# Loading q and k of two blocks in fp32, scores in 64x64 tiles, and a fixed table of orders, in a windowed-attention and SwiGLU kernel

## The chip, the cores and the metric

The kernel runs on one core of one Trainium2 chip. The metric is the device time of one execution in microseconds. It is given as the median of runs, and a profiled execution gives the time and order of every instruction.

## What is computed

```python
# q, k, v: (4, 8, 768, 64) fp32; window = 128, n_sink = 4
scores = (q @ k.T) / sqrt(64)
keep = (key < 4) | ((0 <= query - key) & (query - key < 128))
a = softmax(where(keep, scores, -1e9))
x = (a @ v), heads laid side by side          # 3072 tokens x 512
xn = x / sqrt(mean(x * x) + 1e-6) * rms_g
out = (silu(xn @ w_gate) * (xn @ w_val)) @ w_out   # 512 -> 1536 -> 512
```

## The kernel before

The 768 positions of each of the four batches are cut into six blocks of 128, so that there are 24 blocks g, with t = g % 6 the place in the batch. For a block of 128 keys, the scores are made transposed, keys on the partitions, against the 256 queries of the block itself and the next one: `scores(g)` (line 457) issues eight matmuls of 256 columns, one for each head, two heads at a time on the upper and lower 64 rows of the array. The last block of a batch (`scores_last`, line 475) has 128 columns only. ScalarE takes the exponent out of PSUM (`exps`, line 510), VectorE multiplies by a 0/1 mask (`mask_dve`, line 522, two instructions per block of 128x1024 elements) or, from block 16, GpSimd selects (`mask_pool`, line 535). Blocks 0 and 1 get their mask as a matmul into PSUM beforehand (`mask_bias`, line 447). The sinks are scored for several blocks at once in four column tiles of 32 (`sink_s`, line 668). `av` (line 548) multiplies by v, with a column of ones that gives the sums; `normal`, `square` and `rms` (lines 575 to 616) normalise. x is transposed by TensorE for the first eight blocks and by DMA after.

The FFN takes groups G of four blocks (512 tokens). Group 0 is cut in four chunks of 128 tokens, groups 1 and 2 in two of 256, the others are whole. `ffn` (line 938) issues the gate and value matmuls of one chunk and one set of feature tiles, 16 or 8 or 4 matmuls each, about 0.87 us; ScalarE and VectorE make the hidden tile; `project` (line 892) multiplies by w_out.

q and k of block 0 come in fp32 by SyncE and are cast on the chip. All other q, k, v and all weights are cast by DMAs that GpSimd issues, in the order of `LOADS` (line 186): q and k of block 1, v of block 0, two weight loads, and so on.

What runs when on each engine is set at build time. Every step is registered by `op` with its engine, cost, needs and PSUM banks, and `Plan.run` (line 70) simulates the engines with these costs and always takes the step that can start first. On the chip the five engines then run their lists in order and wait for one another by semaphores. 30 matmuls on zeros (`warm`) are fillers that the planner puts where TensorE has nothing else.

Of the kernel before, what the change touches and what calls it, by code (L numbers as in the profile page):

```python
# [25 lines left out]

class Plan:
# [6 lines left out]
    RESERVE = 8  # L34
# [15 lines left out]
    def land(self, ring, first, work):  # L50


        r = self.rings
        if ring == "POOL":
            begin = max(first, r["POOL"], r["HW"])
            r["POOL"] = begin + (1.4 * work if begin < 8500 else work)
            self.loads -= 1
            return r["POOL"] + 520
        if ring == "HW":
            begin = max(first, r["HW"])  # L60
            r["HW"] = begin + (1.25 * work if begin > 2500 else work)
            return r["HW"] + 900
        begin = max(first, r["TR"], r["POOL"])
        if self.loads:
            r["POOL"] = max(r["POOL"], first) + work
            work *= 2
        r["TR"] = begin + work
        return r["TR"] + (350 if ring == "TR" else 650)

    def run(self):  # L70
        free, users = dict(self.START), {}
        self.loads = sum(o["ring"] == "POOL" for o in self.ops)
        wait = {o["at"]: set(o["needs"]) for o in self.ops}
        cand = {e: [] for e in free}
        left = len(self.ops)
        for o in self.ops:
            for t in o["needs"]:
                users.setdefault(t, []).append(o)
            if not o["needs"]:
                for e in o["ways"]:  # L80
                    cand[e].append(o)
        busy, warm, mode, order = [], False, 0, []
        while left:
            first = None

            many = min(
                (o for o in cand["PE"] if len(o["takes"]) > self.RESERVE), default=None,
                key=lambda o: o["prio"],
            )
            for e, found in cand.items():  # L90
                for o in found:
                    k = len(o["takes"])
                    if k > len(self.banks):
                        continue
                    ready = o["ready"] + self.HOP[e] if o["ready"] else 0
                    if k:
                        ready = max(ready, sorted(self.banks.values())[k - 1] + 40)
                    start = max(free[e], ready)
                    if (k and many and o["prio"] > many["prio"] and start > many["ready"]
                            and len(self.banks) - k < len(many["takes"])):  # L100
                        continue
                    key = (start, o["prio"], ready, o["at"])
                    if first is None or key < first[0]:
                        first = key, e, o
            if first is None:
                raise RuntimeError("stuck: %s" % [
                    (o["gives"], list(wait[o["at"]])) for o in self.ops if o["at"] in wait
                ][:20])
            (start, *_), e, o = first
            for x in o["ways"]:  # L110
                cand[x].remove(o)
            wait.pop(o["at"])
            left -= 1
            ns, lat, fn = o["ways"][e]
            if e == "PE":
                busy = [(a, d) for a, d in busy if a > start - 3413]
                warm = start - free[e] < 4000 and (warm or sum(d for a, d in busy) > 3000)
                ns = ns if warm else 2 * ns
                if o["mode"] != mode:
                    ns, mode = ns + 110, o["mode"]  # L120
                busy.append((start, ns if mode != 2 else 0))
                lat = ns + 180
# [6 lines left out]
            if o["ring"] is not None:  # L129
                end = self.land(o["ring"], end, o["work"]) + self.LATE  # L130
            for s in o["drops"]:
                self.banks[self.held[s]] = end + 12
            for t in o["gives"]:
                for x in users.pop(t, ()):
                    x["ready"] = max(x["ready"], end + 12)
                    w = wait[x["at"]]
                    w.discard(t)
                    if not w:
                        for way in x["ways"]:
                            cand[way].append(x)  # L140
            order.append((start, end, e, fn, o))
        return order


@with_exitstack
def kernel(
# [30 lines left out]
    HW = 4 * VW  # L177
    SW = P // HP
    inv_sqrt_d = 1.0 / math.sqrt(D)
    F32_LOADS = ("ks0","qs0")  # L180
# [4 lines left out]
    DEPTH = 8  # L185
    LOADS = "q-1 k-1 v-0 w-0-2 v-1 qkv-2 qkv-3 w-2-4 w-4-6 w-6-8 w-8-9 w-9-10 w-10-12 qkv-4 wo-0-6 qkv-5 wo-6-12 qkv-6 qkv-8 qkv-7"
    LOADS += "".join(f" qkv-{g}" for g in range(9, NB))
    PE_MASKS = 2
    POOL_MASK_FROM = 16
# [73 lines left out]
    dve(130, lambda: nc.vector.memset(bias.bitcast(I32), 0), gives=["bias0"], prio=-98)  # L263
    for b in range(B):
        dve(60, lambda b=b: nc.vector.memset(V16[b][:, :, :, D:VW], 1.0),
# [49 lines left out]
    dve(220, cut_ident, ["ident"], ["idnos"], -59)  # L315
    dve(700, make_masks, [("bias", 0), ("bias", 1)], ["masks"], MASKS_PRIO)
    dve(300, make_sel, ["ident"], ["sel", "headm"], MASKS_PRIO + 1)
# [27 lines left out]
    for i, name in enumerate(F32_LOADS):  # L345
# [3 lines left out]
           (), [(n + "st", g)], -90 + i, ring="HW", work=970)  # L349
# [10 lines left out]
    def sw_load(fn, gives, work, ns=870, needs=()):  # L360
        n = len(issue)
        more = [("sw", n - DEPTH)] if n >= DEPTH else []
        op({"POOL": (ns, 1900, fn)}, list(needs) + more, list(gives) + [("sw", n)], -89 + n,
# [3 lines left out]
    def sw_block(g, what="qkv"):  # L367
        for n in what:
            needs = [("s", g - LOAD_LEAD)] if g >= LEAD_FROM else []
            if n == "v":  # L370
                sw_load(lambda g=g: load_v(g), [("v", g)], 910, needs=needs)
# [29 lines left out]
    def warm(i):  # L401
        ps = bank(("warm",)) if i == 0 else BANK[("warm",)]
        nc.tensor.matmul(out=ps[:, 0:P], lhsT=zeros, rhs=zeros, start=True, stop=True)

    for i in range(WARM):
        pe(55, lambda i=i: warm(i), ["zeros"] + ([("warm", i - 1)] if i else []),
           [("warm", i)], 1e9, takes=[("warm",)] if i == 0 else (),
           drops=[("warm",)] if i == WARM - 1 else ())
# [7 lines left out]
    pe(1000, unit_gb, ["ones", "grow"], ["gbm"], GB_PRIO, takes=[("gb",)], mode=2)  # L416
# [71 lines left out]

    def exps_last(g, hi):
        if ("el", g) not in T:  # L490
            T["el", g] = epool.tile([P, H, P], BF16, name="e0", bufs=3)
        nc.scalar.activation(
            out=T["el", g][:, hi * HP:(hi + 1) * HP, :].rearrange("p x c -> p (x c)"),
            in_=BANK.pop(("s", g, hi)), func=ACT.Exp, scale=inv_sqrt_d,
        )

    def mask_dve_last(g, hi):
        ev = T["el", g][:, hi * HP:(hi + 1) * HP, :]
# [4 lines left out]
    def mask_pool_last(g, hi):  # L503
        ev = T["el", g][:, hi * HP:(hi + 1) * HP, :]
# [5 lines left out]
    def exps(g, u, hi, n0, n1, last):  # L510
        if ("e", g, u) not in T:
            T["e", g, u] = epool.tile([P, 4, 2, P], BF16, name=f"e{u}", bufs=3)
        ps = BANK[("s", g, u, hi)]
        if last:
            BANK.pop(("s", g, u, hi))
        nc.scalar.activation(  # L516
            out=T["e", g, u][:, 2 * hi:2 * hi + 2, n0:n1, :].rearrange("p x n c -> p x (n c)"),
# [4 lines left out]
    def mask_dve(g, u):  # L522
        t = g % NT
        nq = 2 if t + 1 < NT else 1
        et = T["e", g, u]
        m = masks[:, 0 if t == 0 else 1, 0:nq, :]
        if nq == 2:
            ev = et.rearrange("p x n c -> p x (n c)")
            mv = m.rearrange("p n c -> p (n c)").unsqueeze(1).to_broadcast((P, 4, nq * P))
        else:  # L530
            ev = et[:, :, 0, :]
            mv = m.to_broadcast((P, 4, P))
        nc.vector.tensor_tensor(out=ev, in0=ev, in1=mv, op=ALU.mult)  # L533

    def mask_pool(g, u, n):
        et = T["e", g, u][:, :, n, :]
        if n == 0:
            nc.gpsimd.affine_select(  # L538
                out=et, in_=et, compare_op=ALU.is_ge,
                fill=0.0, base=0, pattern=[[0, 4], [1, P]], channel_multiplier=-1,  # L540
            )
        else:
            nc.gpsimd.affine_select(
                out=et, in_=et, compare_op=ALU.is_ge,
                fill=0.0, base=-1, pattern=[[0, 4], [-1, P]], channel_multiplier=1,
            )

    def av(g, u):
# [7 lines left out]
        for j in range(2):  # L556
            for hi in range(2):
                h = 4 * u + 2 * j + hi
                x = 2 * hi + j
                dest = pv[:, (h - 4 * u) * VW:(h - 4 * u + 1) * VW]  # L560
                if t >= 1:
                    nc.tensor.matmul(  # L562
                        out=dest, lhsT=T["e", g - 1, u][:, x, 1, :],
# [3 lines left out]
                own = (T["e", g, u][:, x, 0, :] if t + 1 < NT  # L567
                       else T["el", g][:, hi * HP + 2 * u + j, :])
                nc.tensor.matmul(  # L569
                    out=dest, lhsT=own, rhs=V16[b][:, t, h, :],  # L570
                    start=(t == 0), stop=True, skip_group_check=True,
                )
        T.pop(("e", g - 1, u), None)

    def normal(g, u):
        if u == 0:
# [127 lines left out]
    def block_scores(g):  # L704
# [10 lines left out]
        for n0, n1 in parts:  # L715
            needs = [("kT", g)] + [("qT", g + i) for i in range(n0, n1)] + gate_of(g)
            needs += [("mb", g)] if g < PE_MASKS else []
# [20 lines left out]
            for u in range(2):  # L738
                for hi in range(2):
                    act(215 * (n1 - n0) + 55,  # L740
                        lambda g=g, u=u, hi=hi, n=(n0, n1), last=last: exps(g, u, hi, *n, last),
                        [("s", g, n0), "table"] + ([("av", g - 2, u)] if g >= 2 else [])
                        + ([("x", g, u, 0, n0)] if hi else []),
                        [("x", g, u, hi, n) for n in range(n0, n1)], early,
                        drops=[("s", g, u, hi)] if last else ())
        for u in range(2):
# [3 lines left out]
            elif g < POOL_MASK_FROM or t == 0:  # L750
                dve(600 if nq == 2 else 335, lambda g=g, u=u: mask_dve(g, u),
                    sum(xs, []) + ["masks"], [("e", g, u)], early)
                es = [[("e", g, u)]] * nq
            else:
                es = []
                for n in range(nq):
# [268 lines left out]
```

## Time and profile before

| | us |
|---|---|
| Runs (3) | 245.65, 244.9, 246.14; median 245.65 |
| Span of the profiled execution, first to last instruction (the only time that its page gives) | 243.9 |
| TensorE busy | 235.3 |
| VectorE busy | 181.1 |
| ScalarE busy | 131.2 |
| GpSimd busy | 89.5 |
| DMA, share of 16 engines' span: GpSimd's queue, SyncE's queue | 80.6%, 28.6% |

The granted TensorE clock is 1.000 over the span. A span of an engine's instruction includes its pipeline: matmuls overlap, so that their busy time is a union and not a sum of column times. PE is TensorE, PEld its weight loads, DVE VectorE, ACT ScalarE, POOL GpSimd, SP SyncE.

### The profile page before, as it was taken

To read this page: it belongs to the slowest core of one execution; us is meant where nothing else is said; L and a number is where in the kernel's file an instruction comes from. 1 tells how busy PE (TensorE), PEld (TensorE's weight loads), DVE (VectorE), ACT (ScalarE), POOL (GpSimd) and SP (SyncE) were. 2 spreads that over 40 slices of the span, in tenths; PEclk is the share of its full clock that TensorE was granted. 3 is DMA by queue.
4 is the path that set the end of the run, shared out by engine and by line. 5 is a ranking of instruction groups with operands and counts; after the bars stand their busy time and mean duration, and the time that the engine had idled before them with its cause. 6 is when DMAs were issued, how large, how long until landed. Compare 5 with 4: busy or idle time off the path is not lost.

```text
span 243.9 us, 5513 instructions
## 1 busy us (share of the span) xinstructions
PE 235.3 (96%) x2116; PEld 148.4 (61%) x2116; DVE 181.1 (74%) x481; ACT 131.2 (54%) x268; POOL 89.5 (37%) x116
## 2 busy tenths in 40 slices
PE   4988999999999999999999999999999999999994
PEld 2558987884788875587786544544554444444443
DVE  4279979896999999999899789896379760377700
ACT  4686565769684827584844574572553311333111
POOL 8976785596435546344520130321320000000000
PEclk9999999999999999999999999999999999999999
DMA  9999999999999999999999461110231002200022
GB/s 127 151 167 196 186 187 187 159 133 163 141 194 162 155 154 156 162 225 137 128 131 143 110 171 25 22 22 21 91 108 24 1 0 86 86 3 0 0 86 86
DMA packets 113579, 27.35 MB, mean 112 GB/s; under 512 B 103697, under 2 KB 110609, under 8 KB 113554
## 3 DMA queue, kind: packets, MB, share of 16 engines
q0 software_dynamic: 81760, 13.90, 80.6%
q1 hardware_dynamic: 31650, 12.99, 28.6%
q8 instruction: 16, 0.26, 0.4%
q10 hardware_dynamic: 144, 0.13, 0.2%
q14 instruction: 9, 0.07, 0.1%
HBM read 28.31 MB, written 6.29 MB: 142 GB/s over the span
## 4 chain that ended last, share of the span: by engine, by line
PE 76%; DMA 15%; DVE 4%; POOL 2%; issue 1%; POOLq 0%
PE v L863 23%; PE g L863 22%; PE o L896 20%; DMA wv<-in_moe_w_val_dram 7%; DMA q<-in_q_dram 5%; PE s L468 3%; DMA v<-in_v_dram 3%; PE av L569 2%; PE av L562 1%; PE av L552 1%; PE o_last L914 1%; DVE e L533 1%; DVE x L581 1%; POOL wg L381 1%; POOL wv L381 1%
## 5 line engine op out<-in xcount | busy, mean ns | idle before, releaser
L863 PE MATMUL v<-xnt,wv 128*128 128x128 bf16 (+2 forms) x528 | 71.1, 282 | 0.0
L863 PE MATMUL g<-xnt,wg 128*128 128x128 bf16 (+2 forms) x528 | 69.8, 282 | 0.3 <-DMA wg<-in_moe_w_gate_dram 0.2
L870 ACT ACTIVATE th<-g 128x512 bf16<-128x512 f32 x72 | 43.2, 600 | 50.0 <-PE g L863 47.4
L896 PE MATMUL o<-wo,hT 128*128 128x512 bf16 x276 | 65.4, 379 | 0.0
L876 DVE SCALAR_TENSOR_TENSOR p<-th,g 128x512 bf16<-128x512 bf16 x72 | 47.9, 682 | 21.6 <-ACT th L870 21.4
L863 PEld LDWEIGHTS <-wg 128*128 128x128 bf16 x528 | 43.1, 98 | 19.7 <-DMA wg<-in_moe_w_gate_dram 0.6
L863 PEld LDWEIGHTS <-wv 128*128 128x128 bf16 x528 | 43.1, 98 | 19.2 <-issue 0.5
L886 DVE TENSOR_TENSOR hT<-p,v 128x512 bf16<-128x512 bf16 x72 | 47.1, 680 | 1.5 <-PE v L863 0.7
L516 ACT ACTIVATE e<-s 128x512 bf16<-128x512 f32 (+1 forms) x88 | 43.8, 569 | 7.2 <-PE s L468 5.8
L896 PEld LDWEIGHTS <-hT 128*128 128x128 bf16 x276 | 25.3, 98 | 26.5 <-issue 1.5
L904 ACT ACTIVATE osb<-o 128x512 f32<-128x512 f32 x23 | 13.8, 601 | 23.4 <-PE o L896 23.4
L335 POOL DMA_DIRECT2D k<-in_k_dram x23 | 20.4, 886 | 16.3 <-DMA v<-in_v_dram 11.3
L339 POOL DMA_DIRECT2D v<-in_v_dram x24 | 21.3, 886 | 11.6 <-DMA q<-in_q_dram 10.5
L335 POOL DMA_DIRECT2D q<-in_q_dram x23 | 20.5, 891 | 11.7 <-DMA k<-in_k_dram 4.0
L581 DVE TENSOR_TENSOR x<-av,rden 128x256 bf16<-128x256 f32 x48 | 20.4, 424 | 1.7
L589 ACT ACTIVATE sq<-x 128x512 bf16<-128x512 bf16 x24 | 15.1, 630 | 11.4 <-DVE x L581 11.3
L613 DVE SCALAR_TENSOR_TENSOR xr<-x,r,gb 128x512 bf16<-128x512 bf16 x24 | 18.0, 751 | 0.9
L533 DVE TENSOR_TENSOR e<-e,masks 128x1024 bf16<-128x1024 bf16 x26 | 17.0, 684 | 1.4 <-ACT e L516 1.4
L538 POOL TENSOR_SCALAR_AFFINE_SELECT e<-e 128x512 bf16<-128x512 bf16 x10 | 6.4, 637 | 31.6 <-ACT e L516 16.1
L569 PE MATMUL av<-v,e 128*128 128x65 bf16 x192 | 17.1, 193 | 0.4 <-ACT e L516 0.3
L562 PE MATMUL av<-v,e 128*128 128x65 bf16 x160 | 15.1, 193 | 0.0
L569 PEld LDWEIGHTS <-e 128*128 128x128 bf16 x192 | 13.0, 97 | 3.3 <-ACT e L516 0.7
(75 smaller groups left out, 181.1 us busy)
## 6 DMA issues: line engine op xcount, KB each, us to landing
out_dram<-osb SPq DMA_DIRECT2D x23, 256.0 KB, 2.3
v<-in_v_dram POOLq DMA_DIRECT2D x24, 128.0 KB, 11.7
q<-in_q_dram POOLq DMA_DIRECT2D x23, 128.0 KB, 12.5
k<-in_k_dram POOLq DMA_DIRECT2D x23, 128.0 KB, 11.8
wo<-in_moe_w_out_dram POOLq DMA_DIRECT2D x2, 768.0 KB, 11.1
wg<-in_moe_w_gate_dram POOLq DMA_DIRECT2D x5, 256.0 KB, 7.7
wv<-in_moe_w_val_dram POOLq DMA_DIRECT2D x5, 256.0 KB, 8.1
stage<-in_k_dram SPq DMA_DIRECT2D x1, 256.0 KB, 3.3
```

The costliest lines, as they stand in the source:

```text
L335: nc.gpsimd.dma_start(out=T[name, g], in_=block_of(src, g))
L339: nc.gpsimd.dma_start(out=V16[b][:, t, :, 0:D], in_=block_of(v, g))
L516: nc.scalar.activation(out=T["e", g, u][:, 2 * hi:2 * hi + 2, n0:n1, :].rearrange("p x n c -> p x (n c)"), in_=ps.rearrange("p (j c) -> p ...
L533: nc.vector.tensor_tensor(out=ev, in0=ev, in1=mv, op=ALU.mult)
L569: nc.tensor.matmul(out=dest, lhsT=own, rhs=V16[b][:, t, h, :], start=(t == 0), stop=True, skip_group_check=True,)
L581: nc.vector.tensor_tensor(out=T["x16", g][:, 4 * u:4 * u + 4, :], in0=pvv[:, :, 0:D], in1=rden.unsqueeze(2).to_broadcast((P, 4, D)), op=AL ...
L613: nc.vector.scalar_tensor_tensor(out=T["xr", g], in0=T.pop(("x16", g)).rearrange("p h d -> p (h d)"), scalar=r[:, 3:4], in1=gb, op0=ALU.mu ...
L863: nc.tensor.matmul(out=ps[:, i * n:(i + 1) * n], lhsT=w_sb[:, kt, ft * P:(ft + 1) * P], rhs=T["xnt", G][:, kt, cols], start=(kt == 0), sto ...
L870: nc.scalar.activation(out=T["th", key], in_=BANK[("g", key)], func=ACT.Tanh, scale=0.5,)
L876: nc.vector.scalar_tensor_tensor(out=T["p1", key], in0=T.pop(("th", key)), scalar=1.0, in1=BANK.pop(("g", key)), op0=ALU.add, op1=ALU.mult,)
L886: nc.vector.tensor_tensor(out=T[hk][:, i:i + n, cols], in0=T.pop(("p1", key)).rearrange("p (n c) -> p n c", n=n), in1=BANK.pop(("v", key)) ...
L896: nc.tensor.matmul(out=BANK[("o", G, tb)], lhsT=T["h", G, ft // 4][:, ft % 4, tb * P:(tb + 1) * P], rhs=wo[:, ft, :], start=(ft == 0), sto ...
```

## The change

Five things change.

1. q and k of blocks 0 and 1 are loaded in fp32, k by SyncE's queue and q by ScalarE's, and cast on the chip. GpSimd no longer loads q and k of block 1.
2. For blocks g >= 4 that are neither first nor last of their batch (13 of them: 4, 7 to 10, 13 to 16, 19 to 22), the scores are made in 64x64 tiles. Keys 0 to 63 of the block need queries 0 to 191, keys 64 to 127 need queries 64 to 255; the last 64 queries of these are put where the first 64 of the others would be. So a head takes three matmuls, of 192, 64 and 128 columns, and ScalarE reads 384 columns per bank instead of 512. The masks put the moved part in its place: two VectorE instructions per block (128x512 and 128x1536), or four GpSimd selects.
3. One tile `e` holds the exponents of all eight heads of a block, where there were two, and a third kind for the last blocks.
4. The order of each engine's steps is read from a table, `ORDER`, in place of the planner's choice. The planner still hands out PSUM banks, with other costs.
5. Each of the 30 fillers takes a bank of its own for itself.

```diff
-    F32_LOADS = ("ks0","qs0")
+    F32_LOADS = ("ks0", "qa0", "ks1", "qa1")
...
-    LOADS = "q-1 k-1 v-0 w-0-2 v-1 qkv-2 qkv-3 w-2-4 w-4-6 ..."
+    LOADS = "v-0 w-0-2 v-1 qkv-2 qkv-3 w-2-4 w-4-6 ..."
+    TRI_FROM = 4
...
+    def tri_scores(g):
+        b, t = divmod(g, NT)
+        qkT = T["qkT", b]
+        for hp in range(HP):
+            u, j = divmod(hp, 2)
+            for kh, c0, q0, n in ((0, 0, 0, TW), (1, 0, TW, DH), (1, DH, DH, P)):
+                for hi in range(2):
+                    pr = slice(hi * D, (hi + 1) * D)
+                    slot = ("s", g, u, hi)
+                    if slot not in BANK:
+                        bank(slot)
+                    k0, q1, o = t * P + kh * DH, t * P + q0, j * TW + c0
+                    nc.tensor.matmul(
+                        out=BANK[slot][kh * DH:(kh + 1) * DH, o:o + n],
+                        lhsT=qkT[pr, 1, hp, k0:k0 + DH], rhs=qkT[pr, 0, hp, q1:q1 + n],
+                        start=True, stop=True, tile_position=(hi * D, kh * DH),
+                        skip_group_check=True,
+                    )
+
+    def tri_exps(g, u, hi):
+        x = HP * hi + 2 * u
+        nc.scalar.activation(
+            out=e_tile(g)[:, x:x + 2, 0:TW],
+            in_=BANK.pop(("s", g, u, hi))[:, 0:2 * TW].rearrange("p (j c) -> p j c", c=TW),
+            func=ACT.Exp, scale=inv_sqrt_d,
+        )
+
+    def tri_mask(g):
+        et = e_tile(g)
+        m = masks[:, 1].rearrange("p n c -> p (n c)")
+        for out, in0, in1 in (
+            (slice(TW, 2 * P), slice(0, DH), slice(TW, 2 * P)), (slice(0, TW),) * 3,
+        ):
+            nc.vector.tensor_tensor(
+                out=et[:, :, out], in0=et[:, :, in0],
+                in1=m[:, in1].unsqueeze(1).to_broadcast((P, H, in1.stop - in1.start)),
+                op=ALU.mult,
+            )
...
+        elif t and g >= TRI_FROM:
+            tri_block(g)
         else:
             block_scores(g)
...
-    order = plan.run()
+    order = plan.run(ORDER)
```

(DH is 64 and TW is 192.) The table counts the steps in the order of their registration. Read back into names, it begins so, with mb for the mask bias, T for a transpose, S for scores (S0.0 and S0.1 against the block itself and the next), VS for a sink product, AV for the two halves of the value product, X for the transpose of x:

```
PE:   7 fillers, mb0, gain broadcast, Tq0, Tk0, filler, Tq1, filler, S0.0, S0.1, filler, Tk1,
      2 fillers, Tq2, filler, AV0.1, VS0.0, filler, AV0.0, mb1, Tq3, filler, S1.0, S1.1, 2 fillers,
      VS0.1, filler, Tk2, 3 fillers, AV1.1, X0, AV1.0, filler, S2, gate 0-3 of chunk 0, sink scores,
      3 fillers, value 0-3 of chunk 0, X1, Tk3, ...
ACT:  load q0, load q1, activation table, cast q0, gain, copy Tq0, copy Tq1, exps of block 0, ...
DVE:  constants, masks, cast k0, cast q1, copy Tk0, cast k1, copy Tk1, copy Tq2, ...
POOL: identity, bias, k2, q2, v0, q3, v1, gate 2-3, value 0-1, gate 0-1, value 2-3, k3, v2,
      gate 6-7, gate 4-5, value 6-7, value 4-5, the other weights up to value 8, q4, q5, k4, v3, ...
SP:   gain row, load k0, load k1, ...
```

## The prediction

> **What bounds the kernel now.** First the page's busy times, then the same by stage, then the timeline of the first 34 us, then the chain of waits.
>
> ```profile
> PE 235.3 (96%) x2116; PEld 148.4 (61%) x2116; DVE 181.1 (74%) x481; ACT 131.2 (54%) x268; POOL 89.5 (37%) x116
> ```
>
> TensorE is busy for 96% of the span, but starts are overlapped and ends modelled, so I ask where its work is thin:
>
> ```profile
> 0.00:6.00 6.00, 2.87 (x14) 1.59 (x15) 2.73 (x16) 2.46 (x3) 4.79 (x11) 1.00 1.02 127
> 6.00:12.00 6.00, 6.00 (x42) 3.64 (x40) 1.52 (x4) 3.73 (x12) 5.98 (x8) 1.00 1.69 151
> 12.00:18.00 6.00, 4.95 (x78) 3.50 (x77) 4.21 (x18) 4.88 (x16) 4.57 (x7) 1.00 2.18 165
> 18.00:24.00 6.00, 5.32 (x95) 4.59 (x94) 5.46 (x16) 4.14 (x11) 3.97 (x6) 1.00 1.45 197
> 24.00:36.00 12.00, 11.74 (x203) 10.98 (x200) 9.74 (x22) 6.59 (x13) 9.57 (x12) 1.00 1.70 187
> ...
> 60.00:80.00 20.00, 20.00 (x212) 15.80 (x210) 19.18 (x52) 14.04 (x31) 9.01 (x11) 1.00 1.87 171
> 80.00:100.00 20.00, 20.00 (x196) 13.60 (x194) 18.86 (x55) 12.09 (x26) 11.37 (x13) 1.00 1.87 157
> ```
>
> Columns: stretch, length, busy time and instructions of PE, PEld, DVE, ACT, POOL, then clock, DMA share, GB/s. PE is full from about 24 us; VectorE is at 94 to 96% between 60 and 100. The thin part is the start: 14 matmuls in 6 us, then 42 and 78. Listing the distances between matmul starts after 46 us, I find none that exceeds the streaming of its columns by more than 0.17 us; nearly all of the excess is 0.09 to 0.11 us on each side of a change of the array's shape. So two things can move the end: when the start fills PE, and how much PE work there is.
>
> ```profile
> 7.24 2.07 PE L411 MATMUL gb<-grow,ones 1*128 1x512 f32 x2
> ...
> 9.24 1.04 PE L468 MATMUL s<-qkT 64*128 64x128 bf16 x16
> ...
> 11.37 1.39 PE L450 MATMUL s<-bias,ident 128*128 128x512 bf16 x4
> ...
> 12.59 0.42 PE L569 MATMUL av<-v,e 128*128 128x65 bf16 x8
> ...
> 17.06 0.40 PE L628 MATMUL x<-ident,xr 128*128 128x128 bf16 x4 [0.61 <-DVE xr L613]
> ```
>
> Columns: start, length in us, engine, line, operation, count. Block 0's scores wait behind the gain broadcast at 7.24, its value product (12.59) behind block 1's mask bias (11.37), and the transpose of x for block 0 comes at 17.06. The first FFN group starts at 19.69.
>
> ```profile
> 15.69 8.13 DMA wv<-in_moe_w_val_dram
> ...
> 24.11 8.46 DMA wv<-in_moe_w_val_dram
> ...
> 65.48 0.22 PE ss L671 x4
> ...
> 80.84 0.33 PE s L484 x8
> ...
> 91.05 0.54 PE s L468 x8
> ```
>
> The chain says the same: until 32.57 (24.11 + 8.46, the last gate and value weights land) it runs through DMAs, then through PE to 240.57. The last 3.3 us (output half, VectorE copy, store) the change leaves alone.
>
> **The change, part by part.** *Start, block 0.* The new PE table puts the gain broadcast and mask bias before the transposes of q and k of block 0, and block 0's value product before block 1's bias. It can: POOL makes the identity and the bias before any load (here one load issue of 1.01 us comes first, and the identity only at 2.42), so that block 0's mask bias, here at 4.16, can start near 2.5. That takes 2.07 us (7.24 to 9.24) out from between the transposes and the scores, and 1.2 us (11.37 to 12.59) out from before the value product. Against it: the gain row goes first on SP and holds k0's issue for 0.47 us; DVE casts q1 before it copies k0's transpose, so block 0's scores wait behind q1's landing, with four fp32 loads in flight. In this trace the first four loads (k0, q0 by SP, q1, k1 by POOL) land at 4.15, 5.42, 6.30 and 7.08, about 1.0 us each; I take the fourth near 7.5 and the first scores near 8.8, 0.4 us earlier instead of 2. The value product then follows the scores by some 2 us (one half's exps, 4 x 0.4 us on ACT) instead of 3.35, near 10.9, 1.7 us earlier; x of block 0 shifts from 17.06 to about 15.4 and the FFN's input to about 16.8.
>
> *Start, weights.* The four weight loads of columns 0 to 4 land, by the trace, at 11.20, 12.53, 19.80 and 21.23, behind ten q, k, v loads on POOL and two on SP. The new table has five on POOL and four on the hardware queues ahead, three blocks fewer. The six blocks between 13.65 and 18.84 took 0.87 us each, so the fourth lands near 18.6 and the third near 17.3. The first FFN group starts at about 17.4, 2.3 us earlier. But all weights land behind eleven blocks instead of twelve: 32.57 becomes about 31.7, 0.9 us earlier, and the new order can run 12 FFN groups before it needs that one, as many as ran by 32.62 here. So the lead carried past the weights is between 0.9 and 2.3 us; I take 1.4, nearer the lower end, since the weights bind last. Below nothing: if four fp32 loads at once push q1 and k1 back by 2 us, the lead is lost, 0. The casts add two VectorE copies of about 0.6 us (the ACT cast is 0.618); they lie in the stretch where VectorE is busy 1.52 of 6 us. ACT's two DMA issues (0.45 to 0.56 each on SP) come before its 1.28 us table load and end near 3.1, before any data lands at 4.15: nothing. What is late next if the cover fails is the copy of k0's transpose.
>
> The Trainium skill, page "DMA: Bandwidth & Descriptors" (section "Issuing engines are not separate DMA queues"), says that issuing on two queues saves issue time alone, because all share the same 16 engines. By it the two-queue part would be worth nothing in transfer time. No run here has two hardware queues loading at once, and the sum above takes nothing from the second queue.
>
> *Scores in 64x64 tiles.* Thirteen blocks (4, 7 to 10, 13 to 16, 19 to 22) go from 8 matmuls of 256 columns to 24 of 192, 64 and 128. The chain prices the old form: 0.54 us with its change of shape, and 0.33 for 8 matmuls of 128 columns. So 128 columns in each of four pairs cost 0.21 us and the fixed part is 0.12. If the two column halves run side by side, each pair takes 192 columns: 0.12 + 0.315 = 0.435, which saves 0.105 per block, 1.4 us for thirteen. If they run one after the other it is 384 columns: 0.12 + 0.63 = 0.75, a loss of 0.21, 2.7 us. Nearest row: the sink scores put four 32-wide column tiles of 256 columns through in 0.22 us, where one after another would be 0.42. Column tiles do run side by side, so I take -1.4.
>
> The Trainium skill, page "TensorE: Matmul & The Clock Gate" (sections "LDWEIGHTS" and "Weight-path perf modes"), speaks against it: fast weight load needs 128 weights, and a plain load takes columns/1.2 ns. With 64-wide tiles that would be 53 ns for each of three loads per half and pair, an estimate of 160 ns where 192 columns stream in 80: the change would cost some 2.9 us more instead of saving. The sink rows show one load per tile, hidden, and no repeated ones, so no row here tests it.
>
> *Beside PE.* The exps of these blocks shrink from 512 to 384 columns: 0.607 to about 0.50 us (0.400 for 256), 52 of them, some 5 us on ACT, which waited 47.4 us for PE: no gain. The two 1024-wide masks (0.684 each) become 512 and 1536: 0.417 + 0.95 = 1.37, as before. POOL's selects stay 512 wide and four per block, two of them now behind a first. Warm fillers stay 30. Together nothing, as long as the table keeps PE fed.
>
> Sum: -1.4 - 1.4 = -2.8 us on the profiled span of 243.9, so 241.1. The runs' median lies 1.75 above that span (launch and end around it), so the time is 242.8.
>
> **The rivals.** *The table starves PE* (the slower side). PE takes its instructions in the table's order, and an entry whose data is late holds all behind it. A middle block's mask is now one step for all eight heads, and the first value product waits for 1.37 us of mask where 0.684 was enough. With VectorE at 95%, the eight blocks masked there could each hold PE for up to 0.7 us: 5.5 us, less 2.8, gives 248.4. It decides from about 0.35 us per block. For it: for 10 us around 93 to 102 the chain runs through VectorE, and PE lost 0.17 us there. Against: PE had FFN work between, and the table places at least one group between most scores and value products.
>
> *Column halves do not overlap* (or weight loads bind): +2.7 - 1.4 = +1.3, 246.9; with half of it 245.6. For: 24 matmuls and 24 weight loads in 0.32 us have no row; against: the sink rows.
>
> *The loads do not get earlier*, four fp32 blocks take what POOL's took and only the tiles gain: -1.4, 244.2. Or the tiles gain nothing and the start does: also 244.2.
>
> **How the numbers follow.** A measurement of this kernel can tell about 0.5%, 1.23 us: faster is below 244.4, slower above 246.9. Forecast (241.2 to 243.8) 0.55; a start better than worked out, below that, 0.03; half of the gain (243.8 to 244.9) 0.16, half of it faster; halves that do not overlap (244.9 to 247.5) 0.10, seven tenths of it same; a starved PE (246.9 to 250) 0.16. Faster 0.66, same 0.15, slower 0.19. The range goes from 240.9 to 247.2, with about 0.12 above and 0.06 below; the forecast's own is 241.2 to 243.8.
>
> **What would show it.** Right: the first FFN group near 17.4 us, the last weights near 31.7, the scores' step at 0.43 to 0.45 us in the chain, no PE distance above 0.3 us after 46. Wrong: a first FFN group after 19; a scores' step above 0.54; VectorE or the e tiles ending PE's waits between 50 and 170 us.

## The result and the profile after

The changed kernel takes 248.08 us in the median of four runs (246.59 to 249.5), the kernel before 245.55 on the same chip: a ratio of 1.0106, 95% interval 1.0075 to 1.0138. It is slower by 1.1%, where 242.8 was forecast. The profiled execution took 246.59 us, its span is 244.9. In the experiments below, two single runs stand above the others of their kernel (250.98 and 273.49 us, with the planner and with pairs and one select) and are left out of the ratios.

The same views as before, first the busy times, then the stages (stretch, length, busy time and instructions of PE, PEld, DVE, ACT, POOL, clock, DMA share, GB/s):

```profile
PE 234.3 (96%) x2298; PEld 150.1 (61%) x2324; DVE 187.1 (76%) x485; ACT 121.4 (50%) x266; POOL 88.3 (36%) x114
```

```profile
0.00:6.00 6.00, 4.87 (x16) 1.88 (x17) 1.99 (x14) 2.05 (x3) 5.06 (x11) 1.00 0.78 147
...
12.00:18.00 6.00, 5.75 (x87) 4.01 (x86) 5.12 (x23) 5.25 (x16) 3.61 (x5) 1.00 1.68 187
18.00:24.00 6.00, 5.68 (x104) 5.48 (x104) 5.75 (x18) 2.86 (x7) 3.70 (x5) 1.00 1.53 193
...
48.00:60.00 12.00, 11.09 (x138) 7.55 (x138) 10.11 (x33) 8.71 (x19) 9.71 (x12) 1.00 2.85 139
60.00:80.00 20.00, 19.89 (x274) 15.94 (x275) 18.72 (x52) 12.77 (x32) 9.36 (x12) 1.00 1.90 157
80.00:100.00 20.00, 18.39 (x184) 13.18 (x186) 17.65 (x52) 10.26 (x24) 10.06 (x12) 1.00 1.84 152
```

The start is fuller (104 matmuls from 18 to 24 us, where there were 95), but PE, which was full from 60 to 100 us, now lacks 0.9 us between 48 and 60 and 1.6 us between 80 and 100. The timeline of the start shows the gain:

```profile
3.74 2.07 PE L466 MATMUL gb<-grow,ones 1*128 1x512 f32 x2
...
8.00 1.25 PE L523 MATMUL s<-qkT 64*128 64x128 bf16 x16
...
15.17 0.40 PE L720 MATMUL x<-ident,xr 128*128 128x128 bf16 x4 [0.24 <-DVE xr L705]
...
16.49 1.07 PE L991 MATMUL g<-xnt,wg 128*128 128x128 bf16 x16
```

The first FFN group starts at 16.49 us, 3.2 us earlier. Counting the column time of the matmuls begun so far and comparing equal amounts in both traces, the changed kernel leads by 2.3 us at 18 us and still by 2.2 at 50. (Such a lead is good to about 0.5 us: it depends on how the work is counted, and 26 matmuls are missing from this trace, which has 2298 of them to 2324 weight loads.) The view of PE's waits shows where that goes; the line names what PE did, what ended the wait, the total, the count and the longest:

```profile
PE s L601 <- DMA qkT<-k: 1.4, 1, 1.4
PE s L601 <- DMA qkT<-q: 0.9, 1, 0.9
PE v L991 <- DMA wv<-in_moe_w_val_dram: 0.5, 1, 0.5
PE g L991 <- DVE hT L1014: 0.4, 2, 0.3
```

Before, the same view has no line at all after 46 us. The two long waits are for DMA transposes, of block 8's q and block 13's k. The chain of waits, in order of time, runs through the second one:

```profile
65.35 0.47 PE s L601 x16
...
77.67 6.75 DMA q<-in_q_dram
84.42 8.69 DMA qkT<-k
93.15 0.54 PE s L601 x16
```

and SyncE's timeline says why it is late:

```profile
79.74 1.19 SPq L497 DMA_TRANSPOSE qkT<-k  x1
81.02 1.23 SPq L497 DMA_TRANSPOSE qkT<-q  x1
...
84.42 2.12 SPq L497 DMA_TRANSPOSE qkT<-k  x1
```

The issue at 84.42 is block 13's k. Block 13's k itself had landed at 77.11. In the table's SP list its transpose stands behind those of block 14's k and q (79.74 and 81.02), the first of which waits for block 14's k to land at 79.72, and behind a store and a transpose of x. It lands at 93.11, 8.7 us after its issue, and the scores start at 93.15. (The load of q that the chain shows before it is block 16's, which was under way at the time; this transpose does not need it.) Of the lead, 1.5 us remain at 80 us and minus 0.45 at 94. A second fall comes between 128 and 186 us, from +0.5 to -1.3, in steps of 0.1 to 0.4 us that end with VectorE; the chain runs through VectorE there for most of 124 to 160.

Over the eight runs of this kernel in two groups, four show a mean granted clock of 0.992 or 0.993 and spans of 246.8 to 247.8 us, four a clock of 0.999 or 1.000 and spans of 244.9 to 245.7. That is some 2 us more in half of its runs; no run with the lower clock was profiled.

### The profile page after: what moved, and what is told of

The parts are those of the page before. It is cut to its first block, busy times and chain, and to the rows that moved or that the text cites. A ratio compares the mean times of both kernels' runs of the same rounds, so it can differ in the third digit from the quotient of the medians.

```text
span 244.9 us, 5831 instructions
## 1 busy us (share of the span) xinstructions
PE 234.3 (96%) x2298; PEld 150.1 (61%) x2324; DVE 187.1 (76%) x485; ACT 121.4 (50%) x266; POOL 88.3 (36%) x114
## 4 chain that ended last, share of the span: by engine, by line
PE 54%; DMA 25%; DVE 12%; POOL 3%; issue 2%; ACT 1%; DVEq 0%; ACTq 0%
PE o L1024 16%; PE v L991 16%; PE g L991 15%; DMA q<-in_q_dram 8%; DMA wv<-in_moe_w_val_dram 7%; DMA qkT<-q 4%; DMA qkT<-k 4%; DVE p L1004 3%; DMA v<-in_v_dram 3%; DVE r L701 2%; DVE xr L705 2%; DVE hT L1014 2%; PE s L601 2%; DVE x L673 1%; PE av L659 1%
## 5 line engine op out<-in xcount | busy, mean ns | idle before, releaser
L991 PE MATMUL g<-xnt,wg 128*128 128x128 bf16 (+2 forms) x521 | 70.7, 281 | 0.8 <-DVE hT L1014 0.4
L998 ACT ACTIVATE th<-g 128x512 bf16<-128x512 f32 x72 | 41.5, 600 | 45.5 <-PE g L991 41.5
L1014 DVE TENSOR_TENSOR hT<-p,v 128x512 bf16<-128x512 bf16 x72 | 48.0, 682 | 15.2 <-PE v L991 12.8
L635 POOL TENSOR_SCALAR_AFFINE_SELECT e<-e 128x512 bf16<-128x512 bf16 x20 | 13.0, 670 | 50.8 <-ACT e L610 44.8
L610 ACT ACTIVATE e<-s 128x384 bf16<-128x384 f32 x52 | 22.9, 499 | 6.2 <-PE s L601 6.1
L391 POOL DMA_DIRECT2D k<-in_k_dram x22 | 19.6, 892 | 12.4 <-DMA v<-in_v_dram 9.3
L391 POOL DMA_DIRECT2D q<-in_q_dram x22 | 19.4, 881 | 11.5 <-DMA k<-in_k_dram 6.4
L705 DVE SCALAR_TENSOR_TENSOR xr<-x,r,gb 128x512 bf16<-128x512 bf16 x24 | 19.5, 812 | 1.1 <-DVE r L701 0.3
L659 PE MATMUL av<-v,e 128*128 128x65 bf16 x192 | 17.4, 195 | 0.1
L574 ACT ACTIVATE e<-s 128x512 bf16<-128x512 f32 (+1 forms) x36 | 15.3, 519 | 1.4 <-PE s L523 1.2
```

What stands on the lines that cost most here:

```text
L391: nc.gpsimd.dma_start(out=T[name, g], in_=block_of(src, g))
L574: nc.scalar.activation(out=e_tile(g)[:, x:x + 2, n0 * P:n1 * P], in_=ps.rearrange("p (j c) -> p j c", c=256)[:, :, n0 * P:n1 * P], func=AC ...
L610: nc.scalar.activation(out=e_tile(g)[:, x:x + 2, 0:TW], in_=BANK.pop(("s", g, u, hi))[:, 0:2 * TW].rearrange("p (j c) -> p j c", c=TW), fu ...
L659: nc.tensor.matmul(out=dest, lhsT=T["e", g][:, x, 0:P], rhs=V16[b][:, t, h, :], start=(t == 0), stop=True, skip_group_check=True,)
L705: nc.vector.scalar_tensor_tensor(out=T["xr", g], in0=T.pop(("x16", g)).rearrange("p h d -> p (h d)"), scalar=r[:, 3:4], in1=gb, op0=ALU.mu ...
L991: nc.tensor.matmul(out=ps[:, i * n:(i + 1) * n], lhsT=w_sb[:, kt, ft * P:(ft + 1) * P], rhs=T["xnt", G][:, kt, cols], start=(kt == 0), sto ...
```

## The experiments

Ratios are to the kernel before, run beside each kernel on its chip; brackets give the 95% interval.

**Block 13's transpose first.** One number moves in SP's list.

```diff
- 22 14 18 314 329 315 330 344 359 345 648 360 643 373 374 395 411 410 658 328 396 653 425
+ 22 14 18 314 329 315 330 344 359 345 648 360 643 373 374 395 396 411 410 658 328 653 425
```

> One number of SyncE's list moves: the transpose of k of block 13 goes ahead of those of block 14, for whose loads SyncE waited (issue at 84.42 us in the changed kernel, landing 93.15, TensorE held 1.5 us at 91.5). Theory A (the table orders DMA transposes and their users too tightly, so TensorE waits): the wait at 91.5 us goes, the time falls by about 1.5 us, to 246.5. Rival B (the loss is VectorE's, late from 120 us on, and a wait before it is given back later): the wait goes but the time stays within 0.5 us of 248.1. Rival C (the loss is a lower TensorE clock in half of the runs, whatever the order): no change in the mean clock.

244.91 us, ratio 0.9979 [0.9959, 0.9999]. SyncE now issues the transpose when block 13's k lands (at 76.89 us here, one line for it and block 14's), and the long wait is gone (a line of PE's timeline, with no idle time ahead of it):

```profile
76.91 4.06 SPq L497 DMA_TRANSPOSE qkT<-k  x2
...
90.50 0.54 PE L601 MATMUL s<-qkT 64*64 64x192 bf16 x24
```

This one order cost 3.1 us in the medians, twice what Theory A expected. 1.45 of it is the wait itself. The lower clock is gone too: ten runs lie between 0.998 and 1.000. Some 1.1 us goes with it, since the changed kernel's eight runs have a median of 248.0 us and its four at full clock one of 246.9. That the wait brought on the low clock is not shown, and a lower mean clock alone is no sign of a longer time: of the 31 runs of the kernel before on this chip, six have 0.992 or 0.993, and their median is 244.6 us against 245.4 for the others. The remaining 0.5 us was not traced. The change is then about as fast as the kernel before, and still 2.1 us above the forecast.

**Block 8's transpose given more time.** On top of the first edit, block 7's scores stand three places later in PE's list.

> As the first, and the scores of block 7 stand three steps later in TensorE's list (behind one output step and both value products of block 6), so that the transpose of q of block 8, which lands at 56.64, is in time. Theory A: 0.9 us more than the first, about 245.6 us, with no wait over 0.4 us between 46 and 120 us; the lead over the kernel before, 2.2 us at 50 us, still stands at 2 us at 100 us. Rival B: the lead is there at 100 us and gone by 190 us, the time near 247.5. Rival C: the runs still split into two groups by their clock.

244.96 us, 0.9995 [0.9976, 1.0013]: nothing gained. The 0.9 us wait is absent, and PE waits 0.5 us for ScalarE's exps in its place. But the 0.9 us wait comes and goes between executions: the profile of the first edit alone does not have it either, nor does the second profile of the changed kernel (below). So this edit had little to win.

**Pairs in place of tiles, nothing else.** In the changed kernel the thirteen middle blocks go back to 8 matmuls of 256 columns, exps of 512 and two masks of 128x1024.

```diff
     def tri_scores(g):
+        scores(g, 0, 2)
...
     def tri_exps(g, u, hi):
+        exps(g, u, hi, 0, 2, True)
...
     def tri_mask(g):
+        for u in range(2):
+            mask_dve(g, u)
...
```

(The lines that these replace, and GpSimd's selects to match, are not shown.)

> The changed kernel and its table, but the scores of the 13 middle blocks come in pairs of 256 columns again, with exponents of 512 and two masks of 1024. By the chain a block's scores took 0.47 us in tiles and 0.54 in pairs. All theories on the order: 0.07 x 13 = 0.9 us slower than the changed kernel, 249.0, if TensorE is what binds. If the waits bind instead (A in its strong form), the waits swallow it: the same time within 0.3 us. Rival D (the tiles themselves cost, by weight loads or banks): faster than the changed kernel.

245.77 us, 1.0029 [1.0004, 1.0055], faster than with tiles, as Rival D had it, though its wait for block 13's k is 1.8 us. The tiles do save on PE (0.47 us in the chain against 0.54), but not at the end. Only one of its ten runs has the lower clock (0.993, 247.91 us), so a wait of this length does not bring that on by itself. At full clock its runs take 244.9 to 246.2 us, those with tiles 246.6 to 247.4.

**The planner in place of the table, all else as changed.**

> All of the change but the table: the planner of before, with its costs for DMAs, chooses each engine's order again; the loads in fp32 and the tiles stay. Theory A: no wait over 0.4 us after 46 us; the tiles give 0.9 us and the start some 1 to 2 us (the first FFN group between 17 and 19 us), so 242.5 to 244.5 us, faster than the kernel before. Rival B (the one mask step for eight heads makes VectorE late in any order): no faster than before, 245.5 or more, with TensorE waiting for VectorE between 120 and 190 us. Rival D: slower than before.

247.27 us, 1.0074 [1.0048, 1.0099]. The first FFN group starts at 20.66 us, the lead is -2.2 us at 18 us and stays between -1.5 and -2.5. The granted clock was 0.54 from 10 to 14 us and 0.50 from 14 to 17 here, which is part of it. So nothing is gained without the table, but the waits for VectorE between 120 and 190 us that Rival B named are not there either.

**The table up to 36 us of the planner's time, then the planner.**

> The changed kernel, but the table is followed only for steps that the planner starts before 36 us; from there the planner of before chooses the order, with the loads in fp32 and the tiles kept. Theory A (the table's first part wins 2 us, its later part gives them back in waits for DMA transposes and VectorE): the lead over the kernel before is 2 us at 36 us and still 2 to 3 us at 220 us; the time is 242.3 to 243.5 us, the fastest so far. Rival B (VectorE is late in any order because of the one mask step for eight heads and a start that comes earlier): the lead falls below 1 us by 190 us, the time is 244.5 or more. Rival E (the start's lead is worth nothing because something else, the loads of later blocks, sets the pace): the lead is gone by 60 us.

252.19 us, 1.0294 [1.0268, 1.0321]. The start is the table's (lead 2.25 us at 18 us), so the start needs the table. After 46 us all is lost, mostly in two waits:

```profile
PE av L712 <- DVE p L1072: 2.4, 1, 2.4
PE ss L831 <- DMA qkT<-q: 2.2, 1, 2.2
```

The forecast that the planner would carry on well from there failed: its choices from a state that it did not make are worse than either whole order. This run prices no part of the change.

**Tiles alone, with the planner and the old loads.**

> The tiles without the loads and without the table: q and k of block 0 by SyncE and of block 1 by GpSimd as before, the planner of before (with the changed kernel's step costs). Theory A: the tiles give 0.07 us on each of 13 blocks, 0.9 us, so 244.3 us against 245.2. Rival B (the one mask step makes VectorE late): 0 or slower, 245.2 or more. Against the run with the planner and the new loads (247.27) this also prices the loads: if that is 2 us slower, the loads in fp32 by themselves cost 2 us in the planner's order.

249.36 us, 1.0167 [1.0149, 1.0185]. The lead falls to -4.8 us by 128. PE's waits name the masks:

```profile
PE av L616 <- POOL e L592: 1.2, 2, 0.8
PE av L616 <- DVE e L579: 1.2, 1, 1.2
```

With the planner, the mask that takes eight heads in one step holds the value products, as the first rival said, and GpSimd's selects hold them as long. These waits are 2.4 of the 4.8 us. In the table these lines are absent.

**The changed kernel again.**

> The changed kernel itself on the same chip, for the spread of its runs and their clock. Theory A: median 246.5 to 248.1, with runs in two groups: those with a mean clock of 1.0 near 246.5, and some with 0.992 about 2.3 us above (half clock for some 4 us), the second group missing in the run that had no wait over 1 us. Rival C (a chip of its own): no run below a clock of 0.998 here, and a median near 246.0.

247.99 us, 1.0104 [1.0075, 1.0133]: the same result in a second set of runs, and two of the four again at a clock of 0.993. The profile has the wait for block 13's k, 1.5 us, and not the one for block 8's q.

**Block 13's transpose first, and pairs.**

> The changed kernel with two edits together: block 13's k transpose ahead of block 14's loads in SP's list, and the thirteen middle blocks' scores again in 8 matmuls of 256 columns (exps of 512, two masks of 1024), all of it in the table's order. Theory A (the 64x64 tiles save their 0.07 us per block on TensorE, 0.9 us, and this reaches the end once the wait at 91 us is gone): slower than with the transpose alone by 0.9 us, 245.6 to 246.0. Theory B (in this order the tiles cost as much as they save, because one mask step for eight heads, or four selects that start together, make the value products late): 244.0 to 244.9, and none of the waits at 127, 146, 158 and 180 us that were left with the transpose alone.

244.42 us, 0.9965 [0.9953, 0.9976]. With pairs it is no slower than with tiles (0.9979): the tiles' saving does not reach the end. The lead is 2.2 us at 46, 2.5 at 178 and 1.5 at 186. So pairs hold the lead through the middle, and 1.0 us goes between 178 and 186.

**Block 13's transpose first, and the mask in halves.** Two steps of 768 and two of 256 elements in place of one of each.

> The changed kernel with block 13's k transpose ahead of block 14's loads, and the mask of the eight blocks that VectorE masks cut into two halves of four heads (two steps of 768 and two of 256 instead of one of each), so that the first value product waits for its own half alone. Theory B (the single step holds the value products): the waits near 127 and 146 us go, 244.3 to 244.7, 0.3 to 0.6 us below the transpose alone. Theory A (the mask is not what is late; VectorE has too much to do there): two more instructions per block cost VectorE some 0.1 us each, 244.9 to 245.4.

245.46 us, 1.0006 [0.9987, 1.0026]. No gain. The wait near 127 us is gone, those near 146 and 158 stay, and this profile has the wait for block 8's q again, 0.6 us. The twelve runs lie in two groups, 244.9 to 245.2 and 245.8 to 246.7 us, and the lower one is no faster than the transpose alone either. So in the table's order the single step for eight heads holds PE by no more than the 0.2 us wait near 127.

**The loads alone, with the planner.**

```diff
-    F32_LOADS = ("ks0","qs0")
+    F32_LOADS = ("ks0", "qa0", "ks1", "qa1")
...
-    LOADS = "q-1 k-1 v-0 ..."
+    LOADS = "v-0 ..."
```

> The kernel before with one edit: q and k of blocks 0 and 1 in fp32 over two hardware queues and cast on chip; scores, masks and the planner as before. Theory A (the loads by themselves make the start earlier): first FFN group near 18 us, 243.7 to 244.7. Theory B (the start's gain is the table's order of the first 20 us, and the loads give it nothing by themselves): first FFN group after 19 us, 245.0 to 247.5.

253.19 us, 1.0333 [1.0304, 1.0361], but this does not price the loads. With v of block 0 first in GpSimd's queue, VectorE's memset of v's column of ones came behind that load, and the bias and the masks stood behind the memset until 9.35 us; PE did its first useful matmul at 10.72:

```profile
9.35 0.10 DVE L265 MEMSET v<- 128x48 bf16 x1 [8.14 <-DMA v<-in_v_dram]
```

The second version has each v load wait for its ones column, as in the changed kernel:

> The kernel before with the fp32 loads of blocks 0 and 1 over two hardware queues and the planner, and each v load made to wait for its ones column (in the run of the loads without that, VectorE stood behind a 128x48 ones column that had to follow the first v load until 9.35 us, and lost 7.5 us by 18 us). Theory A (the loads by themselves make the start earlier): first FFN group at 17 to 18.5 us, 243.4 to 244.5. Theory B (the order of the first 20 us is what gains, the loads alone give nothing): first FFN group after 19.3 us, 245.0 to 247.5.

246.91 us, 1.007 [1.0046, 1.0094]. First FFN group at 19.70 us (19.69 before), lead 0.3 us at 18 and -0.1 at 24. The loads by themselves bring the transpose of block 0's x to 15.25 us (17.06 before), though the clock was 0.53 from 11 to 14.6 us in this profile. But the second gate weights land at 18.38 us, where the changed kernel's order of loads has them at 15.75, and the first FFN group is no earlier. So the 2 us of the start need the order of the first 20 us; whether that order would do without the new loads was not run.

**What takes 1 us between 178 and 186.** With pairs and the transpose in time, once block 22's four GpSimd selects are left out, once VectorE's rms step of block 20 stands one place earlier in its list.

```diff
- ... 541 907 908 922 527 902 ...
+ ... 541 907 908 527 922 902 ...
```

> The version with block 13's transpose first and 256-column pairs, and with block 22's four GpSimd selects left out (its mask is not applied). Theory C (VectorE's steps for block 20's normalised x take 2.9 us instead of 1.8 because these selects run beside them from 176 to 180 us, and that holds the value product and the gate and value matmuls at 180 to 182): xr there back to 0.75 us, the 0.7 us of lead lost between 178 and 186 us kept, 243.6 to 243.9. Rival D (VectorE is late there through its order, not through the selects): 244.2 to 244.6, the waits at 180 and 181 us still there.

> The version with block 13's transpose first and 256-column pairs, and in VectorE's list block 20's rms step one place earlier, ahead of the p step that waits for a tanh until 176 us (VectorE was idle from 171 to 176). Theories C and D both: the rms step runs near 173 us, before the selects, the p steps behind it no longer wait, and the lead lost between 178 and 186 us is kept: 243.5 to 243.9, faster than the kernel before by some 0.6%. Rival (the wait is made by GpSimd's selects being late for the value product itself, or by ScalarE): no change, 244.2 to 244.6.

243.64 us, 0.9925 [0.9906, 0.9944], and 243.59 us, 0.9926 [0.9907, 0.9944]. In both the lead stays at 2.0 us from 182 to the end. Each edit alone brings the whole 0.8 us. So it took both: selects that slow the rms step, and a list that puts the step beside them although VectorE had been idle for 5 us just before. The second is a whole kernel, and the fastest complete one here.

**VectorE's wide mask left out** (tiles, transpose first):

> The changed kernel with block 13's k transpose ahead of block 14's loads, and the 0.96 us mask multiplication over the first 192 columns left out in the eight blocks that VectorE masks (7.7 us off VectorE; those scores go unmasked). Theory E (VectorE's amount of work between 46 and 160 us is what gives back the tiles' 0.9 us): the waits near 127, 146 and 158 us go and the lead stays near 3 us until 178 us: 243.9 to 244.3, some 0.8 us below the transpose alone (244.9). Rival (the tiles lose their 0.9 us in another place, or VectorE's amount does not bind): 244.7 to 245.1.

244.58 us, 0.9975 [0.9956, 0.9993], against 0.9979 with the mask. Theory E falls: 7.7 us less work on VectorE bring nothing. Only the wait near 127 us goes; those at 146 and 158 stay as they were. VectorE is late there for another reason.

**Tiles with both moves, and tiles and pairs with one select of four.**

> The changed kernel, 64x64 tiles kept, with two moves in its table: block 13's k transpose ahead of block 14's loads on SP, and block 20's rms step ahead of the p step that waits for a tanh on VectorE. Theory F (the tiles save 0.07 us per block, and GpSimd's selects, which wait for all eight heads and then run four in a row beside VectorE's rms steps, give it back at 127, 146 and 158 us): within 0.3 us of the same with pairs (243.6), 243.4 to 244.0. Rival A (the tiles' 0.9 us reach the end now): 242.6 to 243.0.

> As the version with tiles and both moves, and of the four GpSimd selects of each of blocks 16 and 19 to 22 only the first is left (the others' masks are not applied). Theory F: the rms steps near 142, 155 and 177 us go back to 1.8 us and the waits at 146 and 158 us go; 242.6 to 243.1, and 0.4 to 0.9 us below the pairs with one select. Rival G (the tiles are worth nothing at the end, whatever the selects do): no less than the pairs with one select, 243.2 to 243.7.

> As the version with 256-column pairs and both moves, and of the four GpSimd selects of each of blocks 16 and 19 to 22 only the first is left (the others' masks are not applied). Both theories: a little below the pairs with all selects, since their trace keeps only 0.1 to 0.2 us of waits there: 243.3 to 243.6. It is the comparison for the tiles with one select.

Tiles 243.89 us, 0.9937 [0.9914, 0.996], no faster than pairs (0.9926). With one select of four, tiles 242.78 us, 0.9896 [0.9871, 0.9921], and pairs 243.4 us, 0.992 [0.9899, 0.9941]. Three selects of four cost the tiles 1.1 us and the pairs 0.2; without them the tiles are ahead by 0.6 us, close to the 0.9 that they save on PE (the two intervals overlap). Up to 128 us the two versions with tiles lead alike, by 2.7 us; at 164 us it is 1.4 with four selects and 2.7 with one. This gap is of one execution each, and part of it is chance: the profile of the first edit alone, whose order is the same up to there, loses 0.5 to 0.7 us in this stretch and not 1.3. PE's waits near 147 and 159 us are there with four selects and gone with one. VectorE's timeline shows why, first with four selects:

```profile
155.93 0.15 DVE L692 TENSOR_SCALAR y<-m 128x1 int32<-128x1 int32 x1
156.12 0.22 DVE L701 SCALAR_TENSOR_TENSOR r<-y,m 128x1 f32<-128x1 f32 x1
156.37 0.57 DVE L701 SCALAR_TENSOR_TENSOR r<-r,y 128x1 f32<-128x1 f32 x1
156.86 0.67 DVE L701 SCALAR_TENSOR_TENSOR r<-r 128x1 f32<-128x1 f32 x2
157.56 1.10 DVE L705 SCALAR_TENSOR_TENSOR xr<-x,r,gb 128x512 bf16<-128x512 bf16 x1
```

and GpSimd in the same execution:

```profile
155.57 2.55 POOL L635 TENSOR_SCALAR_AFFINE_SELECT e<-e 128x512 bf16<-128x512 bf16 x4 [10.64 <-ACT e L610]
```

then VectorE with one:

```profile
154.99 0.16 DVE L694 TENSOR_SCALAR y<-m 128x1 int32<-128x1 int32 x1
155.19 0.22 DVE L703 SCALAR_TENSOR_TENSOR r<-y,m 128x1 f32<-128x1 f32 x1
155.44 0.16 DVE L703 SCALAR_TENSOR_TENSOR r<-r,y 128x1 f32<-128x1 f32 x1
155.51 0.35 DVE L703 SCALAR_TENSOR_TENSOR r<-r 128x1 f32<-128x1 f32 x2
155.90 0.75 DVE L707 SCALAR_TENSOR_TENSOR xr<-x,r,gb 128x512 bf16<-128x512 bf16 x1
```

The one-column step goes from 0.16 to 0.57 us, xr from 0.75 to 1.10; the whole rms takes 2.83 us (155.75 to the next step at 158.58) against 1.76. The pages of the two profiles tell the same of all 24 blocks, first the kernel before, then the changed one. Before, no xr took more than 0.75 us; in the changed kernel four took 1.07 to 1.21:

```profile
L613 DVE SCALAR_TENSOR_TENSOR xr<-x,r,gb 128x512 bf16<-128x512 bf16 x24 | 18.0, 751 | 0.9
L705 DVE SCALAR_TENSOR_TENSOR xr<-x,r,gb 128x512 bf16<-128x512 bf16 x24 | 19.5, 812 | 1.1 <-DVE r L701 0.3
```

With tiles the first select reads all eight heads and waits for all their exps: four then leave in a row. With pairs one starts earlier, and the same rms takes 2.44 us (155.50 to 157.94):

```profile
154.51 0.62 POOL L606 TENSOR_SCALAR_AFFINE_SELECT e<-e 128x512 bf16<-128x512 bf16 x1 [10.42 <-ACT e L574]
155.42 1.81 POOL L606 TENSOR_SCALAR_AFFINE_SELECT e<-e 128x512 bf16<-128x512 bf16 x3 [0.28 <-ACT e L574]
```

So pairs are slowed too. That the earlier start alone makes the difference between 0.2 and 1.1 us at the end is not shown.

The Trainium skill, page "SBUF — State Buffer" (section "SBUF: two separate sides"), has a rule for this: a VectorE operation with two SBUF inputs and a GpSimd operation that reads SBUF exclude one another for a whole instruction. The rows fit it. The slowed steps have two inputs in SBUF, and the extra 0.3 to 0.4 us each are less than one select (0.64 us here); `y`, with one input, keeps its 0.15. The first step of `r` has two inputs as well: it kept its 0.22 us here, and took 0.68 beside the selects at 142 us.

## Why the prediction was wrong

**What failed** is the sentence that priced everything beside PE at nothing, "as long as the table keeps PE fed", with a chance of 0.16 given to the case that it does not. The table did not keep PE fed: PE waited 1.45 us for block 13's k, and moving that one transpose gave 3.1 us. The condition could have been read: the prediction read the table's PE, VectorE and POOL lists for the first 20 us only, and of SP's list the three loads. The order that costs most stands further on in that list. The table's other late step, the rms of block 20 behind a p step, is of the same kind.

**The rival had the right side and the wrong place.** It predicted 248.4 and the time is 248.1, but by VectorE's one mask step in eight blocks. That holds PE under the planner (the tiles-alone run) and not in the table: neither halving the mask nor leaving out its wide part brought anything. That its total came out so near is luck. In place of that mask step stand: block 13's transpose, 3.1 us with the lower clock that went with it; block 20's rms behind the p step, 1.0 us (0.9979 to 0.9937; 0.8 with pairs); and the selects beside the rms steps, 1.1 us (0.9937 to 0.9896). Step by step the change goes from +2.6 us to -0.5, -1.5 and -2.6; the forecast was -2.8. The last version leaves three selects in four out, so it shows where the forecast's time is, and is no kernel.

**Start, -1.4.** Undersized: the lead is 2.3 us at 18 us and 2.2 at 50. First FFN group 16.49 (17.4 forecast), last weights 30.70 (31.7). The part that was taken as binding, the weights behind eleven blocks, came earlier than worked out. The four fp32 loads landed at 4.24, 5.65, 6.65 and 7.95 us, about 1.2 us apart, where the four of before took 1.0: no gain in transfer time from the second hardware queue shows here. That is what the Trainium skill says, page "DMA: Bandwidth & Descriptors" (section "Issuing engines are not separate DMA queues"), and what the sum took.

**Tiles, -1.4.** Oversized: the step is 0.47 us and not 0.435, 0.07 x 13 = 0.9. The column halves do run side by side: one after the other would have been 0.75. 24 loads and 24 matmuls go through in 0.47 us. So the prediction's estimate from the Trainium skill, page "TensorE: Matmul & The Clock Gate" (sections "LDWEIGHTS" and "Weight-path perf modes"), 2.9 us more by plain loads one after another, does not come true here, and the measurement decides.

**Masks and exps.** As worked out: 0.958 + 0.416 = 1.374 us for the two masks against 1.37, exps 0.499. What was missed is that the selects may now only start when all eight heads are done, and what they do to VectorE while they run. "POOL's selects stay" counted their number and not their time.

**The signs named** were good: "no PE distance above 0.3 us after 46" fails at 56, 93 and 130 us and, by less than 0.15 us, from 149 to 183; and "VectorE ending PE's waits between 50 and 170" names the second loss.

## What to carry to other kernels

A change that replaces a planner by a written order has to be read as an order, list by list: for each DMA issue in a queue, what the entry ahead of it waits for, and when the one behind it is needed. Each engine waits in order, so one entry that is a load too early costs more than thirteen blocks save. A step moved beside another engine's work should be priced with that work running, not alone; and a saving on the busiest engine is worth what is left when the next late step has been found, here three times in a row.

## What was not expected of the hardware

GpSimd's selects stretch VectorE's steps with two SBUF inputs, even a step of one column, from 0.16 to 0.57 us.

The clock fell in the middle of a kernel whose TensorE did not stand for more than 2.4 us at a time after its start: in the run with the table up to 36 us, where PE's waits of 2.4 and 0.7 us ended at 89.66 and 91.42. A wait of 2.2 us that ended at 71.82 had no such effect. The columns are those of the stages:

```profile
88.00:91.00 3.00, 1.03 (x18) 0.81 (x18) 2.90 (x8) 0.22 (x1) 1.75 (x2) 1.00 1.70 155
91.00:94.40 3.40, 2.98 (x15) 2.05 (x15) 2.28 (x9) 2.44 (x6) 1.76 (x3) 0.51 2.06 160
```

PE was busy for 1.03 of 3 us, and the next 3.4 us ran at half the clock. Whether the changed kernel's lower clock in half of its runs comes so from its 1.45 us wait is not shown; the version with pairs waits 1.8 us and has it in one run of ten.

The two transposes by DMA that PE waited for took 9.5 and 8.7 us from issue to landing while loads were running, for 2.3 and 2.1 us of issue: here they had to be issued that much ahead.
